# One query range for batch 0 and token groups of 6 and 8 blocks, in a ReLU-squared attention feeding a two-layer expert network

## The chip, the cores and the metric

One core of a Trainium2 chip. The metric is the device time of one execution in microseconds (us). A profile's span is some 1.5 to 2 us shorter than the time of the same kernel, so spans are compared only with spans and times only with times.

## The reference, cut to what matters

```python
batch, n_heads, seq, head_dim = 8, 12, 448, 64          # attention
scores = scale * (q @ k.T);  attn = relu(scores)**2 / S;  o = attn @ v
n_tokens, d_model, d_ff = 3584, 768, 2048               # expert network on the 8*448 tokens
h = x @ w_in;  g = h * sigmoid(1.702 * h);  out = g @ w_out
```

All inputs and the output are float32. The kernel computes in float16 with float32 sums.

Of the kernel before, what the change touches and what calls it, by code (L numbers as in the profile page):

```python
# [15 lines left out]
def kernel(  # L16
# [9 lines left out]
    nc = tc.nc  # L26
    B, H, S, D = q.shape
    NT, DM = out.shape
    DFF = moe_w_in.shape[1]
    J = S // 64  # L30
    NP = H // 4
# [9 lines left out]
    gblk = [4, 8, 8, 8, 6, 8, 6, 8]  # L41
    gcum = [0]
# [93 lines left out]


    def slots_of(q0, n):
        out_ = [[] for _ in range(n)]
        for j in range(J):  # L140
            lo = 0
            while lo < n:
                i, c = divmod(j * n + lo, J)
                hi = min(n, lo + J - c)
                out_[i].append((j, q0 + lo, q0 + hi, 64 * c))
                lo = hi
        return out_

    QA = gblk[0]
    split = slots_of(0, QA) + slots_of(QA, J - QA)  # L150
    whole = [[(j, 0, J, 0)] for j in range(J)]

    def pieces(u):
        return split if u < NP else whole

    early = []

    def scores(u, j, times=1):
        st = units[u]
        sc = early.pop() if early else ps_s.tile([128, 2, 512], F32, name="sc", tag="sc")  # L160
        for kb, q0, q1, c0 in pieces(u)[j] * times:
            for s in range(2):
                for a in range(2):
                    r = slice(64 * a, 64 * a + 64)
                    c = slice(64 * s, 64 * s + 64)
                    nc.tensor.matmul(  # L166
                        out=sc[c, a, c0:c0 + 64 * (q1 - q0)],
                        lhsT=st["kT"][r, kb, c],
                        rhs=st["qT"][r, q0:q1, c],
                        start=True, stop=True)  # L170
        return sc
# [14 lines left out]
    def av_mm(u, j, at):  # L186
        st = units[u]
        if "av" not in st:
            av = ps_s.tile([128, 2, 512], F32, name="av", tag="sc")
            st["av"] = [av[:, 0, :], av[:, 1, :]]  # L190
            st["pair"] = av
        base = QA if u < NP and j >= QA else 0
        for kb, q0, q1, c0 in pieces(u)[j]:
            for s in range(2):
                for a in range(2):
                    r = slice(64 * s, 64 * s + 64)
                    nc.tensor.matmul(  # L197
                        out=st["av"][s][64 * a:64 * a + 64, 64 * (q0 - base):64 * (q1 - base)],
                        lhsT=st["v16"][r, a, 64 * kb:64 * kb + 64],
                        rhs=at[r, a, c0:c0 + 64 * (q1 - q0)],  # L200
                        start=(kb == 0), stop=(kb == J - 1))
# [3 lines left out]
    def xt_evac(u, q0=0, q1=J):  # L205
        b, pr = divmod(u, NP)
        st = units[u]
        lo = b * J + q0
        while lo < b * J + q1:
            g = max(i for i in range(NG) if gcum[i] <= lo)  # L210
            hi = min(b * J + q1, gcum[g + 1])
# [3 lines left out]
            f = slice(64 * (lo - b * J - q0), 64 * (hi - b * J - q0))  # L215
# [204 lines left out]
    with tc.manual_schedule():  # L420
# [34 lines left out]
        def av(how, u, q0, q1):  # L455
            if "m" in how:
                units[u]["av"] = [ps_m.tile([128, 512], F32, name="avm", tag="mm")
                                  for _ in range(2)]
            for jj in range(q0, q1):
                av_mm(u, jj, ats.pop((u, jj)))  # L460
            xt_evac(u, q0, q1)

        def zeros(how, n):
            early.append(ps_s.tile([128, 2, 512], F32, name="sc", tag="sc"))
            for _ in range(n):
# [5 lines left out]
              "a": lambda how, u: av(how, u, 0, J if u >= NP else QA),  # L471
              "b": lambda how, u: av(how, u, QA, J),
# [11 lines left out]
            "jk0 jq0 z3 I jk1 k0 jq1 q0 k1 s0.0 jk2 jq2 s0.1 q1 x0.0 jv0 s0.2 jk4 jv2 k2 x0.1 "  # L484
            "s1.0 jv1 x0.2 jk3 s0.3 jq3 x1.0 s1.1 q2 z3 x0.3 x1.1 jw0 s1.2 s2.0 jv3 s1.3 x1.2 "
            "a0:m x2.0 x1.3 s2.1 s2.2 jw1 x2.1 s2.3 jq4 x2.2 a1:m s1.4 x2.3 s0.4 s0.5 x1.4 x0.4 "
            "a2:m x0.5 s1.5 x1.5 s0.6 jq5 x0.6 f0.0 s2.4 q3 s1.6 x2.4 k3 s2.5 jk5 s2.6:h f0.1 "
            "jw2 f0.2 x1.6 s3.0 x2.5 b1 x2.6 jv4 s3.1 b0:m jw3 x3.0 s3.2 x3.2 s3.3:h f0.3 x3.1 "
            "f0.4 jo0.1 f0.5 s3.4 x3.3 k4 x3.4 s3.5 jo0.0 s3.6 q4 G1 b2 q5 s4.0 jv5 x3.5 f0.6 "
            "x3.6 f0.7 x4.0 s4.1 x4.1 k5 a3 s4.2 f0.8 s4.3 x4.2 x4.3 f0.9 f0.10 L6 s4.4:d s4.5 "  # L490
            "x4.5 jo1.1 x4.4 s4.6:h f0.11 f0.12 s5.0 x4.6 s5.1 x5.0 x5.1 f0.13 a4 s5.2 s5.3:d "
            "f0.14 f0.15 s5.4 x5.3 x5.2 s5.5:d s5.6 x5.4 K6 x5.6 x5.5 m0.1.0 Q6 a5 m0.0.0 f1.0 "
            "f1.1 C1 C3 A2 R6 s6.0:h L7 E3 L8 jo1.0 s6.1 x6.1 A1 s6.2 Q7 C0 f1.2 f1.3 f1.4 s6.3 "
            "K7 C2 f1.5 x6.0 f1.6 R7 A3 f1.7 f1.8 E0 A0 L9 x6.2 x6.3 s6.4 x6.4 s6.5 s6.6 W6 K8 "
            "Q8 B0 B1 x6.5 E1 R8 x6.6 m0.1.1 s7.0 s7.1 B3 x7.0 s7.2 W7 x7.2 x7.1 m0.0.1 s7.3 a6 "
            "K9 s7.4:h x7.3 s7.5 f1.9 B2 s7.6:d f1.10 x7.6 x7.5 f1.11 x7.4 f1.12 s8.0 s8.1:d a7 "
            "s8.2:h Q9 s8.3 x8.0 x8.1 x8.3 W8 f1.13 f1.14 s8.4 R9 s8.5 x8.2 D2 s8.6:h x8.4 L10 "
            "x8.5 f1.15 W9 x8.6 p1.0.0 s9.0 a8 s9.1 E2 s9.2 p1.0.1 f2.0 f2.1 K10 x9.1 x9.0 L11 "
            "Q10 f2.2 x9.2 f2.3 D3 p1.0.2 p1.0.3 s9.3:h s9.4 R10 L12 D0 s9.5 f2.4 x9.4 K11 f2.5 "
            "f2.6 s9.6 Q11 x9.3 R11 x9.5 D1 s10.0:h W10 s10.1 p1.0.4 f2.7 L13 x9.6 f2.8 x10.0 "  # L500
            "x10.1 s10.2:d s10.3 a9 s10.4:h s10.5 x10.2 p1.0.5 x10.3 Q12 p1.0.6 f2.9 x10.4 "
            "x10.5 p1.2.0 p1.2.1 s10.6:d s11.0:h K12 x10.6 s11.1 L14 f2.10 p1.2.2 x11.0 f2.11 "
            "s11.2:d x11.1 a10 s11.3 W11 Q13 f2.12 x11.3 f2.13 x11.2 s11.4 Q14 K13 R12 L15 "
            "s11.5:d s11.6 p1.2.3 R13 p1.2.4 x11.6 x11.5 x11.4 f2.14 f2.15 s12.0 s12.1 a11 "
            "s12.2 K14 L16 p1.2.5 x12.2 p1.2.6 W12 p2.0.0 x12.0 W13 p2.0.1 Q15 x12.1 p2.0.2 "
            "s12.3:d s12.4:d s12.5 x12.3 f3.0 f3.1 f3.2 x12.4 K15 p2.0.3 p2.0.4 s12.6:d x12.5 "
            "L17 s13.0:h R14 s13.1 f3.3 x13.0 x12.6 f3.4 p2.0.5 p2.0.6 x13.1 s13.2 K16 s13.3 "
            "a12 K17 x13.2 W14 s13.4 p2.2.0 p2.2.1 s13.5 s13.6:h x13.3 x13.4 s14.0 x14.0 f3.5 "
            "Q16 p2.2.2 R15 x13.6 f3.6 W15 Q17 x13.5 f3.7 W16 f3.8 s14.1:d L18 a13 s14.2 x14.1 "
            "s14.3:h p2.2.3 f3.9 p2.2.4 x14.2 s14.4 x14.3 s14.5 x14.5 x14.4 R16 s14.6 x14.6 "  # L510
            "f3.10 f3.11 s15.0:d a14 s15.1 s15.2 f3.12 x15.0 Q18 f3.13 f3.14 R17 s15.3 x15.2 "
            "s15.4:h L19 x15.1 s15.5:d p2.2.5 x15.3 p2.2.6 x15.4 s15.6 x15.5 s16.0:h f3.15 f4.0 "
            "x16.0 f4.1 f4.2 f4.3 f4.4 p3.0.0 x15.6 p3.0.1 K18 s16.1:d s16.2:d a15 s16.3 x16.2 "
            "L20 x16.1 f4.5 f4.6 x16.3 f4.7 p3.0.2 s16.4 x16.4 s16.5 Q19 s16.6 f4.8 x16.5 K20 "
            "p3.0.3 s17.0 Q20 s17.1:h x16.6 f4.9 x17.1 f4.10 p3.0.4 x17.0 p3.0.5 W17 s17.2 a16 "
            "s17.3 x17.2 s17.4 f4.11 K19 s17.5:h x17.4 s17.6 x17.3 R18 p3.0.6 p3.2.0 x17.5 L21 "
            "x17.6 p3.2.1 p3.2.2 f4.12 s18.0 s18.1:d s18.2 f4.13 R19 p3.2.3 x18.0 p3.2.4 s18.3 "
            "x18.3 K21 s18.4:h x18.2 x18.1 L22 R20 a17 W18 f4.14 p3.2.5 p3.2.6 s18.5:d s18.6 "
            "f4.15 x18.6 f5.0 x18.5 i4.2.1 f5.1 x18.4 W19 s19.0:d s19.1:d x19.1 s19.2 x19.2 "
            "i4.2.0 K22 f5.2 W20 x19.0 f5.3 s19.3:d a18 s19.4:d s19.5:d Q21 p4.0.0 f5.4 p4.0.1 "  # L520
            "x19.5 f5.5 p4.0.2 Q22 x19.4 x19.3 f5.6 f5.7 s19.6 x19.6 s20.0:d s20.1 x20.0 R21 "
            "f5.8 f5.9 f5.10 s20.2 s20.3:d x20.1 a19 s20.4 x20.3 f5.11 x20.4 R22 p4.0.3 x20.2 "
            "p4.0.4 s20.5:d s20.6 x20.5 x20.6 s21.0:d W21 L23 f5.12 f5.13 s21.1 s21.2:h f5.14 "
            "f5.15 x21.1 x21.0 x21.2 p4.0.5 K23 s21.3 a20 s21.4 s21.5 p4.0.6 p5.0.0 x21.3 f6.0 "
            "f6.1 f6.2 x21.4 s21.6 s22.0:h x21.5 Q23 s22.1 f6.3 x22.1 f6.4 x21.6 f6.5 R23 x22.0 "
            "s22.2 a21 s22.3 s22.4 f6.6 x22.3 p5.0.1 f6.7 W22 f6.8 x22.2 p5.0.2 f6.9 x22.4 "
            "s22.5 x22.5 s22.6 s23.0:d f6.10 p5.0.3 W23 x22.6 p5.0.4 s23.1 s23.2 a22 x23.0 "
            "s23.3:h p5.0.5 x23.1 p5.0.6 s23.4:h x23.2 x23.3 s23.5 s23.6:d f6.11 p5.2.0 x23.6 "
# [41 lines left out]
```

## The kernel before: the parts that the change touches

A "unit" is four heads of one batch; there are 24 units, three to a batch. A "block" is 64 tokens, 7 to a batch, 56 in all. A "slot" is one key block of a unit: four score matmuls on 64x64 tiles of TensorE, a relu (ScalarE, or VectorE where marked `:d`) and a square (VectorE). The expert network runs on groups of blocks. The whole schedule is one list of words, issued in that order on every engine:

- `jk jq jv jw jo`: loads of k, q, v, w_in, w_out through GpSimd's queue; `k q`: transposes on TensorE with a copy on VectorE
- `s u.j`: scores and relu of slot j of unit u (`:t` issues the score matmuls twice, `:h` holds the relu back); `x`: its square; `a`, `b`: a unit's value product and its copy to the token tile
- `z3`: three filler matmuls of zeros; `I`: makes the identity matrix that the transposes need
- `f g.i`: matmuls of w_in for group g; `m`: one direct w_out product of 128 tokens; `p`: a paired product, 7 products of 8 matmuls for two token tiles in place of 8; `i`: the same tile alone; capitals: loads, casts and transposes of later units, and sums of weights

Before, batch 0 is computed in two query ranges, 4 blocks and 3 blocks, so that the first group of 4 blocks is ready early. Its slots are packed from pieces of different key blocks:

```python
gblk = [4, 8, 8, 8, 6, 8, 6, 8]
...
QA = gblk[0]
split = slots_of(0, QA) + slots_of(QA, J - QA)      # 10 + 9 pieces in 4 + 3 slots
whole = [[(j, 0, J, 0)] for j in range(J)]          # 7 pieces in 7 slots
...
for kb, q0, q1, c0 in pieces(u)[j] * times:         # pieces(u): split for units 0 to 2
    for s in range(2):
        for a in range(2):
            nc.tensor.matmul(out=sc[c, a, c0:c0 + 64 * (q1 - q0)],
                             lhsT=st["kT"][r, kb, c], rhs=st["qT"][r, q0:q1, c], ...)
```

Every matmul is two instructions of TensorE, a weight load and the matmul: the page counts 3392 of each.

## Time and profile before

| | before |
|---|---|
| time, median of 4 runs (lowest to highest) | 385.76 us (385.29 to 386.5) |
| span of the profile | 384.3 us |
| TensorE busy, matmuls | 370.9 us, 3392 |
| first expert matmul (word f0.0) starts | 23.80 us |
| clock at half | 24.2 to 27.6 us |
| waits of TensorE before 80 us that the profile names, over 0.8 us each, without the first (1.2 us, for the zeros of the fillers) | weight block 1.1, q of unit 6 0.9, and 1.2 with the cause "issue" |

"Issue" is time in which the engine waited for nothing that the profile shows; the prediction passed over that 1.2 us. It is one line of TensorE's order of time, in the middle of the value product of unit 2:

```profile
19.60 0.81 PE L197 MATMUL avm<-at,v 64*64 64x256 f16 x15
21.62 0.71 PE L197 MATMUL avm<-at,v 64*64 64x256 f16 x25 [1.21 <-issue]
```

(Start, duration, engine, line, operation, count, and in brackets the idle time before it and what ended it.)

### The profile page before, as it was taken

Reading aid. Unit: us, or ns where it says so; the run is one execution under the profiler, and the core shown is the slowest. Engines: PE = TensorE matmul, PEld = TensorE weight load, DVE = VectorE, ACT = ScalarE, POOL = GpSimd, SP = SyncE. Lnnn points to the kernel's source line nnn. Section 1 sums busy time; section 2 is a strip of 40 time slices with the busy share of each in tenths; the row PEclk is TensorE's granted clock in tenths of the full one; section 3 lists DMA queues with packets and bytes.
Section 4 is the critical chain, followed back from the end, with each engine's and each line's share of the span. In section 5 each row is a group of like instructions: output and inputs, shape, how many; then the busy total and the mean of one; then the engine's idle time right before and its main releaser. Section 6 shows DMA issues by size and latency. Waiting matters only on the chain.

```text
span 384.3 us, 8393 instructions
## 1 busy us (share of the span) xinstructions
PE 370.9 (97%) x3392; PEld 196.7 (51%) x3392; DVE 268.4 (70%) x442; ACT 210.4 (55%) x310; POOL 136.0 (35%) x200
## 2 busy tenths in 40 slices
PE   8779999999999999999999999999999999999994
PEld 4557653444545455544455555454455555555552
DVE  2878886797678879786768888587855867023473
ACT  1979855878684673585656755326567450232210
POOL 7618514816433351324433321343324220332100
PEclk9989999999999999999999999999999999999999
DMA  8999998996559878798432399365141331110333
GB/s 117 196 204 158 204 231 242 237 193 143 151 141 224 166 156 218 162 197 146 131 82 97 68 198 275 62 87 143 26 107 24 49 84 39 44 41 0 84 82 83
DMA packets 65222, 50.87 MB, mean 132 GB/s; under 512 B 35744, under 2 KB 61728, under 8 KB 65184
## 3 DMA queue, kind: packets, MB, share of 16 engines
q1 hardware_dynamic: 47872, 35.70, 38.0%
q0 software_dynamic: 17152, 14.55, 25.8%
q8 instruction: 26, 0.43, 0.4%
q10 hardware_dynamic: 160, 0.10, 0.1%
q14 instruction: 12, 0.10, 0.1%
HBM read 45.61 MB, written 11.01 MB: 147 GB/s over the span
## 4 chain that ended last, share of the span: by engine, by line
PE 84%; DMA 9%; DVE 2%; POOL 1%; issue 1%; ACT 1%; SPq 0%; ACTq 0%
PE ht L245 36%; PE op L310 29%; PE sc L166 8%; PE av L197 6%; DMA win<-in_moe_w_in_dram 3%; DMA wout<-in_moe_w_out_dram 3%; DMA qst<-in_q_dram 2%; PE op L271 1%; DVE osb L321 1%; PE zp L428 1%; DMA qT<-q 1%; PE tr L129 1%; ACT rl L180 0%; POOL k L119 0%; PE sc L466 0%
## 5 line engine op out<-in xcount | busy, mean ns | idle before, releaser
L245 PE MATMUL ht<-xt,win 128*128 128x512 f16 (+2 forms) x768 | 156.6, 353 | 1.2 <-DMA win<-in_moe_w_in_dram 1.1
L252 POOL TENSOR_SCALAR gt<-gf 128x512 f16<-128x512 f32 (+2 forms) x128 | 82.8, 647 | 206.4 <-ACT gf L250 200.6
L180 ACT ACTIVATE rl<-sc 128x896 f16<-128x896 f32 x138 | 121.8, 924 | 47.4 <-PE sc L166 38.4
L453 DVE TENSOR_TENSOR at<-rl 128x896 f16<-128x896 f16 x168 | 104.8, 651 | 20.9 <-ACT rl L180 20.1
L250 ACT ACTIVATE gf<-ht 128x512 f32<-128x512 f32 (+2 forms) x128 | 69.8, 547 | 86.4 <-PE ht L245 74.8
L245 PEld LDWEIGHTS <-win 128*128 128x128 f16 x768 | 72.1, 98 | 76.1 <-issue 13.9
L310 PEld LDWEIGHTS <-gt 128*128 128x128 f16 x424 | 40.6, 98 | 29.9 <-issue 3.4
L166 PE MATMUL sc<-qT,kT 64*64 64x448 f16 (+4 forms) x816 | 49.3, 327 | 2.6 <-ACT rl L180 1.0
L310 PEld LDWEIGHTS <-as 128*128 128x128 f16 x320 | 30.8, 98 | 23.5 <-issue 2.8
L310 PE MATMUL op<-wout,as 128*128 128x384 f16 x224 | 40.3, 326 | 0.0
L177 DVE TENSOR_SCALAR rl<-sc 128x896 f16<-128x896 f32 x30 | 32.2, 1085 | 11.1 <-PE sc L166 10.9
L310 PE MATMUL op<-wsum,gt 128*128 128x384 f16 x224 | 39.5, 326 | 0.0
L321 DVE SCALAR_TENSOR_TENSOR osb<-op,osb 128x384 f32<-128x384 f32 (+1 forms) x49 | 25.7, 545 | 14.9 <-PE op L310 14.6
L310 PE MATMUL op<-wout,gt 128*128 128x384 f16 (+1 forms) x200 | 35.3, 320 | 0.5 <-DVE osb L321 0.5
L197 PE MATMUL av<-at,v 64*64 64x448 f16 (+3 forms) x660 | 33.2, 336 | 0.0
L166 PEld LDWEIGHTS <-kT 64*64 64x64 f16 x816 | 19.3, 106 | 26.7 <-issue 20.6
L321 DVE SCALAR_TENSOR_TENSOR osb<-op,ea 128x384 f32<-128x384 f32 x24 | 13.3, 553 | 26.8 <-ACT eb L319 11.3
L217 DVE CAST xt<-av 128x768 f16<-128x768 f32 (+5 forms) x35 | 24.7, 735 | 8.5 <-PE av L197 8.4
L197 PEld LDWEIGHTS <-v 64*64 64x64 f16 x816 | 21.4, 107 | 12.6 <-issue 2.6
L305 DVE TENSOR_TENSOR as<-gt 128x1024 f16<-128x1024 f16 x38 | 26.1, 712 | 0.4 <-POOL gt L252 0.4
L104 POOL CAST q<-qst 128x896 f16<-128x896 f32 x18 | 16.9, 936 | 9.9 <-DMA qst<-in_q_dram 9.1
L91 POOL DMA_DIRECT2D v<-in_v_dram x24 | 18.0, 752 | 1.9 <-issue 0.6
(38 smaller groups left out, 170.0 us busy)
## 6 DMA issues: line engine op xcount, KB each, us to landing
out_dram<-osb SPq DMA_DIRECT2D x54, 192.0 KB, 2.9
kst<-in_k_dram SPq DMA_DIRECT2D x18, 448.0 KB, 4.0
qst<-in_q_dram SPq DMA_DIRECT2D x18, 448.0 KB, 4.7
v<-in_v_dram POOLq DMA_DIRECT2D x24, 224.0 KB, 5.2
win<-in_moe_w_in_dram POOLq DMA_DIRECT2D x8, 384.0 KB, 10.0
wout<-in_moe_w_out_dram POOLq DMA_DIRECT2D x4, 768.0 KB, 12.5
k<-in_k_dram POOLq DMA_DIRECT2D x6, 224.0 KB, 6.1
q<-in_q_dram POOLq DMA_DIRECT2D x6, 224.0 KB, 7.8
```

Source lines behind the costliest of these rows:

```text
L166: nc.tensor.matmul(out=sc[c, a, c0:c0 + 64 * (q1 - q0)], lhsT=st["kT"][r, kb, c], rhs=st["qT"][r, q0:q1, c], start=True, stop=True)
L177: nc.vector.tensor_scalar(out=rl, in0=sc[:, :, 0:S], scalar1=0.0, scalar2=None, op0=ALU.max)
L180: nc.scalar.activation(out=rl, in_=sc[:, :, 0:S], func=AF.Relu)
L197: nc.tensor.matmul(out=st["av"][s][64 * a:64 * a + 64, 64 * (q0 - base):64 * (q1 - base)], lhsT=st["v16"][r, a, 64 * kb:64 * kb + 64], rhs ...
L217: nc.vector.tensor_copy(out=xts[g][:, 2 * pr:2 * pr + 2, c], in_=st["pair"][:, :, f])
L245: nc.tensor.matmul(out=ht[:, 0:n], lhsT=w[:, kk, fo:fo + 128], rhs=xts[g][:, kk, 0:n], start=(kk == 0), stop=(kk == NK - 1))
L250: nc.scalar.activation(out=gf[:, 0:n], in_=ht[:, 0:n], func=AF.Gelu_apprx_sigmoid, scale=1.0 / SC)
L252: nc.gpsimd.tensor_scalar(out=gts[g][:, f, 0:n], in0=gf[:, 0:n], scalar1=SC, scalar2=1.0, op0=ALU.mult, op1=ALU.mult)
L305: nc.vector.tensor_tensor(out=out_, in0=x, in1=y, op=op)
L310: nc.tensor.matmul(out=op[:, 0:cw], lhsT=lhs[:, f, :], rhs=w[:, f, c0:c0 + cw], start=(start and f == 0), stop=(stop and f == HF - 1))
L321: nc.vector.scalar_tensor_tensor(out=o, in0=op[:, 0:w], scalar=sc, in1=add, op0=ALU.mult, op1=ALU.add)
L453: nc.vector.tensor_tensor(out=at, in0=rl, in1=rl, op=ALU.mult)
```

## The change

The intent is a simpler start: batch 0 like all others, in one query range with whole key blocks, and the groups 6, 8, 6, 8 and so on. The first group then needs all of batch 0's attention, less its last block. The list of words is a new one for the whole kernel.

```diff
-    gblk = [4, 8, 8, 8, 6, 8, 6, 8]
+    gblk = [6, 8] * (B // 2)
...
-        for kb, q0, q1, c0 in pieces(u)[j] * times:
-            for s in range(2):
+        for s in [0, 1] * times:
...                                             (the same in av_mm; xt_evac loses its query range)
-            "jk0 jq0 z3 I jk1 k0 jq1 q0 k1 s0.0 jk2 jq2 s0.1 q1 x0.0 jv0 s0.2 jk4 jv2 k2 x0.1 "
-            "s1.0 jv1 x0.2 jk3 s0.3 jq3 x1.0 s1.1 q2 z3 x0.3 x1.1 jw0 s1.2 s2.0 jv3 s1.3 x1.2 "
-            "a0:m x2.0 x1.3 s2.1 s2.2 jw1 x2.1 s2.3 jq4 x2.2 a1:m s1.4 x2.3 s0.4 s0.5 x1.4 x0.4 "
-            "a2:m x0.5 s1.5 x1.5 s0.6 jq5 x0.6 f0.0 s2.4 q3 s1.6 x2.4 k3 s2.5 jk5 s2.6:h f0.1 "
...                                             (35 lines cut)
+            "jq0 jk0 I q0 k0 z3 s0.0:d x0.0 s0.1 x0.1 jq1 jk1 s0.2 q1 s0.3 x0.2 x0.3 s0.4 k1 "
+            "x0.4 z3 jk4 jk2 s0.5 s0.6 k2 k4 x0.5 s1.0 s1.1 jv0 x0.6 s1.2 jq3 x1.0 x1.1 a0:m "
+            "s1.3 s1.4 x1.2 jq2 s1.5 jk3 q2 jk5 x1.3 x1.4 jv2 s1.6 x1.5 jv1 k3 s2.0:t q3 x1.6 "
+            "jw0 s2.1:t x2.1 s2.2:t x2.0 s2.3:t x2.2 a1:m x2.3 s2.4:t jq4 jq5 s2.5:t s2.6 x2.4 "
+            "x2.5 x2.6 jv3 jw1 jv4 k5 s3.0 jv5 a2 s3.1 q4 jw2 x3.0 x3.1 s3.2 f0.0 q5 x3.2 jw3 "
...                                             (34 lines cut)
```

## The prediction

The sum of the forecast came to +1.2 us, so 386.8 us, rounded to 386.5. Its unit costs are read from the trace of the kernel before (512, 384 and 256 columns 0.216, 0.1625 and 0.109 us apart; for the last, twelve take 1.48 us and six 0.83). The 2 us for three relu buffers in step c is the author's estimate, which no row shows.

> **What bounds the kernel now.** I read the page's busy table and slices first, then the stage table, then the order of time on TensorE and on VectorE, and the chain of waits last. "Slot" below means one key block's scores of one unit (four heads of one batch), its relu and its square. There are 24 units of 7 slots.
>
> ```profile
> PE 370.9 (97%) x3392; PEld 196.7 (51%) x3392; DVE 268.4 (70%) x442; ACT 210.4 (55%) x310; POOL 136.0 (35%) x200
> PE   8779999999999999999999999999999999999994
> DVE  2878886797678879786768888587855867023473
> ACT  1979855878684673585656755326567450232210
> PEclk9989999999999999999999999999999999999999
> ```
>
> TensorE is busy for 97% and is full in every slice but the first three and the last. So its work from the fourth slice on is on the path that sets the end, and only the first 30 us, where it has holes, can hide anything. The stage table shows what bounds that first stretch:
>
> ```profile
> core 0: us, PE busy (x) PEld busy (x) DVE busy (x) ACT busy (x) POOL busy (x), PEclk, DMA share, GB/s
> 10.00:20.00 10.00, 7.52 (x253) 5.45 (x249) 9.31 (x19) 9.91 (x14) 6.23 (x9) 1.00 1.25 198
> 20.00:30.00 10.00, 7.71 (x175) 5.55 (x177) 6.97 (x13) 7.61 (x11) 1.58 (x4) 0.83 1.25 205
> 30.00:40.00 10.00, 9.89 (x234) 7.04 (x225) 8.36 (x16) 9.22 (x16) 9.18 (x14) 1.00 1.01 158
> 50.00:60.00 10.00, 9.70 (x86) 5.17 (x84) 8.09 (x15) 3.44 (x5) 1.73 (x3) 1.00 1.00 208
> 60.00:70.00 10.00, 9.14 (x54) 3.84 (x53) 7.35 (x12) 7.51 (x12) 5.92 (x8) 1.00 1.05 265
> ```
>
> From 10 to 20 us ScalarE (9.91 of 10) and VectorE (9.31) are the full ones, with the loads running at about 200 GB/s beside them. From 20 to 30 us TensorE also loses clock (0.83). The chain of waits names the transfers that end last there:
>
> ```profile
> 12.22 11.44 DMA win<-in_moe_w_in_dram
> 23.80 1.13 PE ht L245 x6
> ...
> 48.49 9.56 DMA qst<-in_q_dram
> 58.11 0.94 POOL q L104
> 59.06 2.89 DMA qT<-q
> 62.09 0.76 PE sc L166 x12
> ```
>
> The first expert matmul (word f0.0) starts at 23.80, when the first weight block lands, after a wait of 1.1 us. The next wait is at 62.09: 0.9 us for the transposed q of unit 6.
>
> The unit costs of TensorE come from starts that follow each other in order of time:
>
> ```profile
> 349.23 1.46 PE L245 MATMUL ht<-xt,win 128*128 128x512 f16 x6
> 350.53 1.46 PE L310 MATMUL op<-wout,gt 128*128 128x384 f16 x8
> 351.83 4.05 PE L245 MATMUL ht<-xt,win 128*128 128x512 f16 x18
> ```
>
> Six 512-column matmuls take 350.53 - 349.23 = 1.30 us (0.216 each), and eight 384-column ones 351.83 - 350.53 = 1.30 us (0.1625 each). A whole slot's four 64x448 matmuls cost 0.189 us (the chain has 28 for a unit's value product in 1.32 us), a set of 14 transposes 0.52 us.
>
> [...] the six 256-column matmuls at 23.80 take 1.13 us, against 0.83 us for the six at 41.42, and the granted clock there is 0.83. [...] switches between 64x64 and 128x128 cost about 0.12 us each, worked out below. [...] 24 matmuls of 64 to 192 columns starting at 18.40 take 0.58 us, about 0.1 us for four, and so do four of 256 columns.
>
> **The change part by part.**
>
> *a. The split goes.* Units 0 to 2 did their attention in two query ranges (4 and 3 blocks). The pieces are 10 + 9 = 19 per unit instead of 7, at about 0.105 us: 2.0 us against 7 x 0.189 = 1.32, for scores and again for values. That saves 6 x 0.7 = 4.1 us of TensorE at most. The larger part lies before f0.0, in the holes. Nine of the 21 slots, and the three later value products, lie after it; I count 1.0 us on the path.
>
> *b. Groups 4,8,8,8,6,8,6,8 become 6,8 four times.* The first weight product keeps 3584 x 96 columns. The second pairs token tiles: 56 matmuls for two tiles, against 32 for one done alone. Before: 12 pairs, 2 singles, 2 direct = 672 + 64 + 64 = 800. After: 11 pairs, 3 singles, 3 direct = 616 + 96 + 96 = 808. Eight more at 0.1625 = +1.3 us, on the path.
>
> *c. The first group needs six blocks of batch 0 instead of four*, so all seven key blocks of all seven queries of units 0 to 2. From the listed order, before f0.0 stand 17 slots, 6 transpose sets and three partial value products before, and 24 slots, 11 sets and three whole ones after.
> VectorE sets this start, as an estimate from its rows and their starts. Up to the last copy of unit 2's values it has 21 squares (about 0.556 from start to start) = 11.7; 10 copies of transposes at 0.54 = 5.4; one relu 1.02; two value products copied in two halves of 448 (0.415 at 256 and 0.558 at 384 columns give some 0.535 start to start) = 2.1; one of 896, 1.03. The sum is 21.3 us from 7.59, plus 1.0 of holes seen at the start now: 29.9. ScalarE alone would reach 9.4 + 20 x 0.837 = 26.1, and the weight block (3.77 MB at the rates of the stage table) about 24 to 25. Three relu buffers tie ScalarE and VectorE together, both nearly full; I add 2 us for it. So f0.0 starts at 32, 8.2 us later than now.
> It then has more behind it. Useful TensorE work before f0.0, now: 6 x 0.52 + 17 x 0.189 + 12 slots' values 2.3 = 8.6 us. After: 11 x 0.52 + 24 x 0.189 + 21 x 0.189 = 14.2. Time that is not useful: 23.8 - 8.6 = 15.2 now, 32 - 14.2 = 17.8 after. Net +2.6 us. Doubled score matmuls (six slots marked for it, 1.1 us) lie in the holes and cost nothing.
>
> *d. From f0.0 to the value product of unit 6 (79.58 now).* Useful work now: by 79.58 12 x 0.52, 53 slots' scores and 42 slots' values at 0.189, 96 matmuls of 256 columns at 0.109, 54 at 0.216 and 64 at 0.1625 give 56.7; less 8.6 is 48.1 us, in 55.8. The 7.7 us lost are: the half clock at 23.8 to 28 about 1.6 (1.13 instead of 0.67, and likewise for the next five rows), the split 1.0, the q wait 0.9, and 4.2 of switches. After, the wait should go: the list puts three direct tiles (3 x 2.6 us) and two f words before unit 6's first slot, near 68 us, while its q is ready at about 62 (gate, load, cast and transpose as now). The split's 1.0 goes by (a). The clock dips as now.
>
> *e. Switches.* In 79.6 to 350 us useful work is 260.4 of 270.4, so 10 us are lost over the 80-odd mode switches of the list: 0.12 each. From unit 7's fourth slot on the lists have 84 and 86 switches: no difference. Between f0.0 and there they have 41 and 22, so up to 19 x 0.12 = 2.3 less. I take 0.8 of it, since the first weight blocks, the weight sums and the copies are as likely to open holes in the same stretch.
>
> Sum: +1.3 (b) + 2.6 (c) - 1.0 (a) - 0.9 (d) - 0.8 (e) = +1.2 us. On the measured median 385.6 that is 386.8; I round to 386.5.
>
> **The rivals.**
> 1. *TensorE starves longer at the start.* For: VectorE and ScalarE are already full from 10 to 20 us, and the new list doubles score matmuls from unit 2 on, which only makes sense where TensorE stands waiting. Each us that f0.0 comes after 32 adds nearly one: f0.0 at 37 gives 391 to 392. Against: the holes in ScalarE and VectorE from 20 to 30 us (7.61 and 6.97) show that a denser list has room.
> 2. *The new list is simply tighter.* If VectorE runs as in the sum without the 2 us, all 19 saved switches count, and the doubled scores keep the clock up (1.6), the sum is 386.8 - 2 - 1.5 - 1.6 = 381.7. For: 128 runs of one mode in the list against 135. Against: a denser 30 to 60 us has less slack for late transfers.
> 3. *A transfer takes the place of the wait removed.* The third and fourth w_in blocks are issued behind the first group's activations; I expect them at 37 and 41, used at about 45 and 51. If the order on the queue shifts by some 10 us, a hole of 2 to 3 us appears: 389.
>
> **Range and chances.** The two large unknowns are the start of f0.0 (some 3 us either way) and the holes up to 80 us (2 to 3); the rest of the kernel is the same kind of full TensorE. That gives 382 to 392. Two per cent is 7.7 us: faster would need nearly every loss before 80 us to go (2%), slower a start like rival 1 and a missed transfer (7%), within 91%.
>
> **What would show it.** Step b: 808 matmuls of the second product. Step a: 672 value matmuls, 696 score matmuls. Step c: f0.0 at 30.5 to 33, VectorE over 90% busy before it. Step d: no wait of unit 6's scores for its q. Step e: equal pace from unit 7 on, and the same tail of some 6 us. I am wrong if f0.0 comes after 35, if TensorE has over 3 us of holes between f0.0 and 80 us, or if the later stretch differs by more than 2 us.

## The result, and the profile after

| | before | after |
|---|---|---|
| time, median of 4 runs (lowest to highest) | 385.76 us (385.29 to 386.5) | 382.78 us (382.41 to 383.24) |
| span of the profile | 384.3 us | 380.7 us |
| TensorE's instructions in the program (two for each of 3392 and 3136 matmuls, and two more) | 6786 | 6274 |
| w_out matmuls (the last eight are done as two halves of 192 columns each, counted once here; the trace has 808 and 816) | 800 | 808 |
| f0.0 starts | 23.80 us | 28.60 us |
| clock at half before the end | 24.2 to 27.6 us | never |

The ratio of the times is 0.9922, with a 95% interval of 0.9901 to 0.9942: 0.8% shorter. The time lies in the predicted range, 0.8 us above its lower end, but the forecast leaned to slower and the kernel became faster.

The page of the changed kernel, the same rows as shown of before:

```profile
PE 370.2 (97%) x3136; PEld 193.3 (51%) x3136; DVE 256.5 (67%) x425; ACT 214.6 (56%) x314; POOL 136.0 (36%) x200
PE   8889999999999999999999999999999999999994
DVE  2999763778958986566778874638777865313374
ACT  2987753786776768367564556476764461242210
PEclk9999999999999999999999999999999999999999
```

TensorE is busy for 0.7 us less in a span that is 3.6 us shorter. The work is nearly the same, the holes are fewer. The table by stage (busy us of TensorE, weight loads, VectorE, ScalarE, GpSimd, then the granted clock, the share of the transfer engines, GB/s):

```profile
10.00:20.00 10.00, 8.33 (x159) 4.84 (x158) 9.90 (x21) 9.07 (x12) 6.47 (x11) 1.00 1.23 191
20.00:30.00 10.00, 8.89 (x162) 5.34 (x160) 10.00 (x21) 9.12 (x12) 4.12 (x6) 1.00 1.25 206
30.00:40.00 10.00, 10.00 (x118) 5.12 (x112) 9.06 (x14) 7.74 (x13) 6.40 (x10) 1.00 1.24 205
50.00:60.00 10.00, 10.00 (x80) 5.49 (x79) 4.00 (x7) 3.64 (x7) 4.49 (x7) 1.00 1.20 237
60.00:70.00 10.00, 10.00 (x61) 4.73 (x59) 5.16 (x8) 4.86 (x7) 3.59 (x5) 1.00 0.89 225
```

Compare the second row with before's: VectorE 10.00 in place of 6.97, ScalarE 9.12 in place of 7.61, TensorE 8.89 in place of 7.71 at a full clock in place of 0.83, and 162 matmuls in place of 175. The start is denser on all three, with fewer and larger matmuls. From 30 us on TensorE has no hole in any of these rows. The waits of TensorE that are left:

```profile
PE tr L129 <- DVE xt L197: 1.3, 2, 0.6
PE zp L405 <- DVE zero L402: 1.2, 1, 1.2
PE sc L145 <- ACT rl L159: 0.7, 2, 0.4
PE tr L129 <- DVE kT L133: 0.5, 1, 0.5
PE op L287 <- DVE osb L298: 0.5, 1, 0.5
```

(Who waited for whom; us in total, times, longest.) The waits for the weight block, for unit 6's q and the one without a cause are gone.

The account further down rests on two more readings, with the columns of the table by stage. In the changed kernel VectorE is full from its first relu to f0.0:

```profile
8.25:28.60 20.35, 17.27 (x330) 10.13 (x322) 20.21 (x40) 18.50 (x22) 12.34 (x18) 1.00 1.24 197
```

In the kernel before TensorE is busy for less than half of the time just before its clock falls at 24.2 us:

```profile
20.00:21.00 1.00, 0.41 (x13) 0.25 (x13) 0.94 (x2) 1.00 (x3) 0.00 (x0) 1.00 1.26 205
21.00:22.00 1.00, 0.38 (x24) 0.38 (x27) 0.63 (x1) 0.79 (x1) 0.00 (x0) 1.00 1.23 202
22.00:23.00 1.00, 0.72 (x40) 0.51 (x29) 0.70 (x3) 0.44 (x1) 0.00 (x0) 1.00 1.26 204
23.00:24.00 1.00, 0.20 (x2) 0.22 (x3) 1.00 (x3) 1.00 (x2) 0.00 (x0) 1.00 1.24 204
```

Where the 3.6 us of span came from, with the prediction's own measure, useful TensorE work from the lists at the same unit costs against time gone by:

| stretch | before: time, useful, lost | after: time, useful, lost | lost, difference |
|---|---|---|---|
| start to f0.0 | 23.8, 8.6, 15.2 | 28.6, 14.2, 14.4 | -0.8 |
| f0.0 to unit 6's value product (79.58; 78.53) | 55.8, 48.1, 7.7 | 49.9, 47.3, 2.6 | -5.1 |
| from there to the end | 304.7, 288.4, 16.3 | 302.2, 284.9, 17.3 | +1.0 |
| w_out work (8 more matmuls) | | | +1.3 useful |

The sum is -3.6 us. The last stretch differs by 1.0 us in one profile each, which no run here explains.

### The profile page after: what moved, and what is told of

The parts are those of the page before. It is cut to its first block, busy times and chain, and to the rows that moved or that the text cites. A ratio compares the mean times of both kernels' runs of the same rounds, so it can differ in the third digit from the quotient of the medians.

```text
span 380.7 us, 7864 instructions
## 1 busy us (share of the span) xinstructions
PE 370.2 (97%) x3136; PEld 193.3 (51%) x3136; DVE 256.5 (67%) x425; ACT 214.6 (56%) x314; POOL 136.0 (36%) x200
## 4 chain that ended last, share of the span: by engine, by line
PE 90%; DVE 7%; issue 1%; ACT 1%; ACTq 0%
PE ht L222 39%; PE op L287 29%; PE sc L145 9%; PE av L174 7%; PE op L248 4%; DVE at L430 3%; DVE osb L298 1%; PE zp L405 1%; DVE kT L133 1%; PE tr L129 1%; DVE xt L197 1%; DVE qT L133 1%; DVE rl L156 0%; ACT eb L296 0%; ACT rl L159 0%
## 5 line engine op out<-in xcount | busy, mean ns | idle before, releaser
L222 PE MATMUL ht<-xt,win 128*128 128x384 f16 (+1 forms) x768 | 156.3, 353 | 0.4 <-ACT gf L227 0.4
L229 POOL TENSOR_SCALAR gt<-gf 128x384 f16<-128x384 f32 (+1 forms) x128 | 82.6, 645 | 201.6 <-ACT gf L227 196.5
L159 ACT ACTIVATE rl<-sc 128x896 f16<-128x896 f32 x144 | 126.2, 917 | 41.9 <-PE sc L145 33.5
L227 ACT ACTIVATE gf<-ht 128x384 f32<-128x384 f32 (+1 forms) x128 | 69.6, 546 | 85.9 <-PE ht L222 76.4
L145 PE MATMUL sc<-qT,kT 64*64 64x448 f16 x696 | 48.6, 357 | 1.2 <-ACT rl L159 0.7
L298 DVE SCALAR_TENSOR_TENSOR osb<-op,osb 128x384 f32<-128x384 f32 (+1 forms) x45 | 23.6, 544 | 23.6 <-PE op L287 23.3
L156 DVE TENSOR_SCALAR rl<-sc 128x896 f16<-128x896 f32 x24 | 26.1, 1087 | 16.1 <-PE sc L145 15.8
L174 PE MATMUL av<-at,v 64*64 64x448 f16 x616 | 33.2, 350 | 0.2 <-DVE at L430 0.2
L287 PE MATMUL op<-wout,gt 128*128 128x384 f16 (+1 forms) x184 | 32.4, 319 | 0.5 <-DVE osb L298 0.5
L194 DVE CAST xt<-av 128x896 f16<-128x896 f32 (+2 forms) x32 | 24.5, 793 | 11.6 <-PE av L174 11.6
L145 PEld LDWEIGHTS <-kT 64*64 64x64 f16 x696 | 17.2, 105 | 24.9 <-issue 17.2
L174 PEld LDWEIGHTS <-v 64*64 64x64 f16 x672 | 19.8, 107 | 12.8 <-issue 2.8
L104 POOL CAST q<-qst 128x896 f16<-128x896 f32 x18 | 17.3, 959 | 8.4 <-issue 7.5
```

The source lines that it names most:

```text
L145: nc.tensor.matmul(out=sc[c, a, 0:S], lhsT=st["kT"][r, j, c], rhs=st["qT"][r, :, c], start=True, stop=True)
L156: nc.vector.tensor_scalar(out=rl, in0=sc[:, :, 0:S], scalar1=0.0, scalar2=None, op0=ALU.max)
L159: nc.scalar.activation(out=rl, in_=sc[:, :, 0:S], func=AF.Relu)
L174: nc.tensor.matmul(out=st["av"][s][64 * a:64 * a + 64, 0:S], lhsT=st["v16"][r, a, 64 * j:64 * j + 64], rhs=at[r, a, :], start=(j == 0), st ...
L194: nc.vector.tensor_copy(out=xts[g][:, 2 * pr:2 * pr + 2, c], in_=st["pair"][:, :, f])
L222: nc.tensor.matmul(out=ht[:, 0:n], lhsT=w[:, kk, fo:fo + 128], rhs=xts[g][:, kk, 0:n], start=(kk == 0), stop=(kk == NK - 1))
```

## The experiments

Times below are the mean of a run's fast runs less that of the kernel before in the same rounds; the changed kernel stands at -3.0 us on this scale. The first runs asked which parts of the new start carry the gain: the place of the filler matmuls, the doubled scores, VectorE, the pieces, the groups.

### Fillers ahead of the first transposes again

```diff
-            "jq0 jk0 I q0 k0 z3 ...
+            "jq0 jk0 z3 I q0 k0 ...
```

> The changed kernel, with one thing put back: the three filler matmuls of zeros stand before the first transposes again (and the identity matrix is made between them), as in the kernel before. Theory S (VectorE sets when the first expert matmul f0.0 starts, from its first copy on, and TensorE then runs full to the end): VectorE's first copy starts about 0.8 to 1.0 us later, f0.0 at 29.4 to 29.6 in place of 28.6, and the time is 0.8 to 1.0 us longer than the changed kernel's. Rival R (the start has slack, the gain over the kernel before is less work and fewer mode switches on TensorE): f0.0 moves by less than 0.3 us and so does the time.

Measured: 382.92 us, ratio 0.9926, -2.9 us. f0.0 at 28.61 us. The rival's "no difference" held, but the profile did not test its reason (and the times cannot tell less than their intervals of 0.8 us): VectorE's first copy started at 6.61 us, as in the changed kernel (6.60), and its second at 7.16 (7.14). The second set of transposes waits for the load of k, which landed at 6.27 us here and at 6.30 there, and the fillers cost little here, since TensorE's full clock was granted from 5.0 us on. That instant differs from profile to profile, from 4.3 to 7.1 us (6.44 in the changed kernel's), with no relation to the list that they show. The 7.59 us that the prediction took from the kernel before is a late draw of it: full clock came at 7.09 us there, the three fillers started 0.43 us apart in place of 0.21, and the first transposes, behind them, began at 6.88 us although their load had landed at 5.09, as early as in any profile.

### The doubled scores left out

```diff
-    ... s2.0:t ... s2.1:t ... s2.2:t ... s2.3:t ... s2.4:t ... s2.5:t
+    ... s2.0 ... s2.1 ... s2.2 ... s2.3 ... s2.4 ... s2.5
```

> The changed kernel without the doubling of six score slots of unit 2 (24 matmuls fewer, 1.1 us of TensorE work). Theory C (the doubled scores keep TensorE dense enough that its clock isn't halved when the experts start): the granted clock falls to 0.5 for about 3 us somewhere between 20 and 32 us, as in the kernel before, and the time is 1.0 to 1.6 us longer. Rival (they lie in holes and the clock would hold anyway): clock 1.00 throughout, time within 0.3 us. Third possibility: they are in the way of the start, and without them f0.0 comes up to 0.5 us earlier.

Measured: 383.38 us, ratio 0.9933, -2.5 us; the granted clock is 1.00 in all stages up to the end. In this profile f0.0 came at 29.83 us, after waits of 2.0 us in all for loads of k that the changed kernel's profile does not have. The doublings neither keep the clock up (Theory C, which rested on the one fall at 24.2 us in the kernel before) nor cost anything that these runs can tell from noise (0.5 us between two intervals of 0.8 to 0.9 us half-width).

### Doubled scores in the kernel before

```diff
-    ... s0.4 s0.5 ... s1.5 ... s0.6
+    ... s0.4:t s0.5:t ... s1.5:t ... s0.6:t
```

> The kernel before, with the scores of four slots (units 0 and 1, the last before f0.0) doubled, nothing else. Theory C: TensorE's clock, which falls to 0.5 from 24.4 to 27.4 us, holds at 1.0; the 1.6 us that the six instruction groups of that stretch lost come back, the time is 1.2 to 1.6 us shorter than the kernel before. Rival: the clock falls in spite of it, since the hole of 1.1 us ahead of f0.0 and the one of 1.2 us before it remain, and the time is within 0.3 us.

Measured: 389.38 us, ratio 1.0083, +3.2 us. Neither theory had this time. The clock still fell, as the rival said, but twice (21.8 to 25.2 and 28.6 to 32.0 us), and TensorE stood still twice without a cause in the profile:

```profile
21.88 0.53 PE L166 MATMUL sc<-qT,kT 64*64 64x128 f16 x9 [1.87 <-issue]
28.61 0.31 PE L129 MATMUL tr<-ident,q 128*64 128x128 f16 x1 [1.65 <-issue]
```

The second stop is before the last of 14 transposes whose inputs are the same tile. Data cannot be what the last one lacked. That made a new theory necessary.

### First transposes ahead of the fillers in the kernel before

```diff
-            "jk0 jq0 z3 I jk1 k0 jq1 q0 k1 ...
+            "jk0 jq0 I k0 q0 z3 jk1 jq1 k1 ...
```

> The kernel before, with the first transposes put ahead of the three filler matmuls of zeros, as the changed kernel has them. Theory S says of the kernel before that f0.0 waits there for the weight block's transfer (landed at 23.67), not for VectorE: VectorE's first copy starts 0.8 to 1.0 us earlier, but f0.0 stays at 23.3 to 23.9 and the time moves by less than 0.4 us. Rival: the earlier start by itself is worth what it is worth in the changed kernel, 0.8 to 1.0 us shorter.

Measured: 385.87 us, ratio 1.0003, +0.1 us. f0.0 at 24.17 us after 1.7 us of waiting for the weight block: outside the stated 23.3 to 23.9, but the time did not move, as expected. The order within the first words is worth nothing in either kernel that these runs can tell (0.1 us, with intervals of 0.8 to 1.0 us half-width).

### More work on VectorE

```diff
-            nc.vector.tensor_tensor(out=at, in0=rl, in1=rl, op=ALU.mult)
+            for _ in range(2 if "w" in how else 1):          # x0.4 x1.1 x1.4 x2.1 marked w
+                nc.vector.tensor_tensor(out=at, in0=rl, in1=rl, op=ALU.mult)
```

> The changed kernel, with four of the squares before f0.0 (in units 0, 1 and 2) done twice on VectorE: the same values, 4 x 0.56 = 2.2 us more of VectorE. Theory S (VectorE sets f0.0): f0.0 at 30.4 to 30.9 in place of 28.6 and the time 1.8 to 2.2 us longer. Rival R (ScalarE or the transfers set it, VectorE has slack): f0.0 moves by less than 1 us, and what it moves is made up later; time within 0.5 us.

Measured: 384.98 us, ratio 0.9981, -0.7 us, so 2.3 us more than the changed kernel. f0.0:

```profile
30.86 1.15 PE L222 MATMUL ht<-xt,win 128*128 128x384 f16 x6
```

28.60 became 30.86: 2.26 us later for 2.2 us of added VectorE work, and all of it arrives at the end. VectorE is on the path up to f0.0, and nothing after it absorbs a delay.

### The split's arithmetic in the new order

```diff
+    QA = 4                                         # pieces of 4 and 3 blocks for units 0 to 2, 19 per unit
-        base = QA if u < NP and j >= QA else 0
+        base = 0                                   # both ranges into one tile: VectorE's work is unchanged
```

(On the kernel before, with the new groups and the new list.)

> The changed kernel with the arithmetic of batch 0 in two query ranges again (4 and 3 blocks: 19 pieces per unit and product in place of 7), in the changed order, with the same work on VectorE and ScalarE. It shows what the smaller pieces cost by themselves, about 4 us of TensorE work by my count. Theory S (TensorE has holes before f0.0, and all of it lies there): time longer by 0 to 0.8 us. Rival R (TensorE's work counts there too): 2.5 to 4 us longer.

Measured: 392.67 us, ratio 1.0181, +7.0 us: 10 us more than the changed kernel, with the same list and the same work on VectorE and ScalarE. Both theories are far off; 4 us of array time cannot cost 10. TensorE's order of time has four stops without a cause and f0.0 at 37.80 us:

```profile
15.14 1.30 PE L197 MATMUL avm<-at,v 64*64 64x256 f16 x61 [0.50 <-issue]
...
21.40 0.35 PE L129 MATMUL tr<-ident,k 128*64 128x128 f16 x5 [2.39 <-issue]
...
27.32 1.00 PE L197 MATMUL avm<-at,v 64*64 64x64 f16 x47 [1.15 <-issue]
...
33.26 2.66 PE L197 MATMUL av<-at,v 64*64 64x256 f16 x72 [2.42 <-issue]
...
37.80 1.72 PE L245 MATMUL ht<-xt,win 128*128 128x384 f16 x6
```

Numbering TensorE's instructions in the program and counting the matmuls in the trace up to each stop gives the same place every time: 223 matmuls and instruction 448, 351 and 704, 479 and 960; the fourth stop is at 606 recorded matmuls, two instructions short of 1216, which one missing record explains. These are 192 + 256, + 512, + 768, + 1024. The stop of the kernel before is at instruction 704 too, and so is the first of the kernel before with doubled scores; its second is at 960.

The page has a transfer queue called "instruction". Its line in part 3, of the kernel before and of the changed one:

```profile
q8 instruction: 26, 0.43, 0.4%
```
```profile
q8 instruction: 24, 0.39, 0.4%
```

(Packets, MB, share.) In the trace each packet is 16384 bytes. 6786 and 6274 instructions, less the first 192, are 25.8 and 23.8 times 256, and the queue has 26 and 24 packets: so I read a packet as one block of 256 instructions of TensorE, with the stops at the edges of the blocks. The times of the packets fit:

| split in the new order: packet on the instruction queue | 12.7 to 13.6 | 18.8 to 19.8 | 25.1 to 26.0 | 31.0 to 31.9 |
|---|---|---|---|---|
| TensorE resumes after the stop | 15.14 | 21.40 | 27.32 | 33.26 |

TensorE resumes 1.3 to 1.6 us after each packet has landed. The next packet starts 3.5 to 3.7 us after it resumed. One round is some 6.1 us, and in that time TensorE can use 128 matmuls. In the changed kernel the packet of 22.5 to 23.5 us is landed well before TensorE reaches instruction 704, between 25 us (306 matmuls) and 30 us (392). There, too, the packets start only after TensorE has passed an edge, 2.4 to 2.9 us after it (448, 704 and 960 passed at 19.60, 27.28 and 37.69 us, packets at 22.5, 29.7 and 40.2), so at these three edges the supply is not more than one block ahead. In the kernel before, instruction 704 is reached at 20.4 us, its packet landed at 20.1, and TensorE resumes at 21.62.

Theory I is that reading. The next runs test it.

### Many small matmuls against few large ones

Both without `:t`, in 18 slots before f0.0:

```diff
+        if extra == "y":                       # many: sixteen matmuls of 64 columns, the same values again
+            for s in [0, 1] * 4:
+                for a in range(2):
+                    nc.tensor.matmul(out=sc[c, a, 0:64], lhsT=st["kT"][r, j, c],
+                                     rhs=st["qT"][r, 0:1, c], start=True, stop=True)
```
```diff
+        if extra == "y":                       # few: two matmuls of zeros of 512 columns
+            for a in range(2):
+                nc.tensor.matmul(out=sc[:, a, :], lhsT=zero[:, 0:128], rhs=zero[:, 0:512], ...)
```

> Theory I (new, from the runs so far): TensorE's own instructions come in blocks of 16 KB, 256 instructions, over a transfer queue of their own; while the loads fill the transfer engines a block takes about 6 us to arrive, so TensorE can use at most some 128 matmuls (a weight load and a matmul each) per 6 us, and stands still at the block's edge if it needs more. The split's small pieces do that. Here: the changed kernel without its six doublings, and in 18 of the slots before f0.0 sixteen more matmuls of 64 columns on 64x64 tiles (the same values again), 288 in all or 576 instructions; at about 0.026 us each that is 0.42 us of TensorE a slot, 7.5 us in all. Theory I: stops of 1 to 2.5 us each with no cause in the trace, at instructions 704, 960 and 1216 of TensorE's stream (192 and a multiple of 256), f0.0 at 36 to 39 in place of 28.6, time 8 to 11 us longer than the changed kernel. Rival W (what counts is TensorE's array time): f0.0 at 31 to 33 and no such stops, time as in the next run.

> The same array time in few instructions: the changed kernel without its six doublings, and in the same 18 slots two matmuls of zeros of 512 columns on the whole array (0.43 us a slot, 7.8 us in all, 36 matmuls or 72 instructions). Theory I: no stops without a cause, f0.0 at 29 to 32 (part of the 7.8 us fits into the holes), time 0.5 to 3 us longer than the changed kernel. Rival W: the same f0.0 and time as in the run with many small matmuls, within 1 us.

Measured: many 388.55 us, ratio 1.0067, +2.5 us, f0.0 at 34.96; few 388.15 us, ratio 1.0054, +2.0 us, f0.0 at 34.15. The places of the stops came as Theory I said (instructions 448, 704, 960, and 1216 but for the same missing record), with 1.55, 2.32, 0.99 and 1.33 us; the few large matmuls have none. The times missed, and f0.0 with them, on both sides: 5.5 us more than the changed kernel for the many in place of 8 to 11, and 5.0 for the few in place of 0.5 to 3. The large ones filled TensorE itself (10.00 busy of 10 from 10 to 30 us), so only some 2 to 3 of their 7.8 us fitted into holes. And a small matmul takes far less array time than the 0.026 us I had assumed, an estimate (a quarter of the prediction's 0.105 us per piece of four matmuls); in the next run 128 of them take 1.24 us, 0.0097 each. So this pair shows where the stops come from, but its times do not tell the theories apart.

### Instructions alone, with the transfer engines idle

```diff
+        for _ in range(225):                   # after the last word: 900 matmuls of 64 columns
+            for s in range(2):
+                for a in range(2):
+                    nc.tensor.matmul(out=bt[c, a, 0:64], lhsT=ident[r, c], rhs=ident[r, 0:64], ...)
```

> The changed kernel with 900 matmuls of 64 columns on 64x64 tiles after everything else, when the loads are long over and only the last store is in flight: 1800 instructions, seven blocks. It measures how fast TensorE's instructions can arrive when nothing else uses the transfer engines. Theory I: blocks follow each other by less than 4.5 us, and each stop at a block's edge is under 1 us or there is none[...]. Rival (a block takes some 6 us whatever the load): 7 blocks x 6 = 42 us or more.

Measured: 402.81 us in one look. TensorE's order of time at the end:

```profile
375.82 2.19 PE L520 MATMUL burst<-ident 64*64 64x64 f16 x147
379.32 1.24 PE L520 MATMUL burst<-ident 64*64 64x64 f16 x128 [1.30 <-issue]
383.32 1.72 PE L520 MATMUL burst<-ident 64*64 64x64 f16 x128 [2.76 <-issue]
387.05 1.93 PE L520 MATMUL burst<-ident 64*64 64x64 f16 x128 [2.01 <-issue]
390.78 1.92 PE L520 MATMUL burst<-ident 64*64 64x64 f16 x128 [1.80 <-issue]
```

Exactly 128 matmuls from stop to stop, with no load and no wait; the last stores end at 380 us, so from the second stop on hardly anything else moves. Rounds of 3.5 to 4.0 us, so the stated "under 4.5" held and "6 us whatever the load" is out; the stops are 1.3 to 2.8 us, longer than stated, since 128 of these matmuls run in 1.24 us at the full clock. So the supply of TensorE's instructions is one block per 3.7 us or so when the transfer engines are idle, and one per 6.1 us during the loads of the start. The packets show where the difference lies: a packet takes 0.9 to 1.4 us in both cases, and TensorE resumes 1.3 to 1.6 us after it has landed, but it starts 1.0 to 1.7 us after TensorE resumed here, and 3.5 to 3.7 us after it under the loads.

### The split with fewer loads

```diff
+        if u >= NP:                            # load16: batch 1 takes the tiles of batch 0 (wrong result)
+            st[n + "16"] = units[u - NP][n + "16"]
+            return
-    ... jw1 ... jw2 ... f0.0 q5 ...
+    ... f0.0 jw1 jw2 q5 ...
```

> The kernel with the changed order and the split arithmetic (the one that stopped at 19.0, 26.1 and 30.9 us and started f0.0 at 37.8), with fewer loads: batch 1's q and k are not loaded (its units take the tiles of units 0 to 2, so the result is wrong on purpose), and the second and third weight block are asked for only after f0.0. The transfer engines then run dry from some 22 us until f0.0. Theory I: the stops after 22 us shrink to under 0.5 us or vanish, f0.0 at 29 to 33. Rival (the stops come from the small pieces themselves or from the sequencer): stops at the same instructions, of the same length, f0.0 after 35.

Measured in one look, with a wrong result on purpose: f0.0 at 33.30 us, just outside the stated 29 to 33, in place of 37.80. The transfer engines fell to 44 GB/s from 20 to 30 us. The stops at 448 (0.40 us) and 704 (2.29 us) are there as before, when the loads still ran; at 960 and 1216 there are none. The packets, 5.8 us apart until 19.0, follow then at 22.6, 26.9 and 30.7 us, 3.6 to 4.3 apart. Same instructions, same pieces, no stops once the loads are gone: it is the supply under load. (The clock was at half from 20.7 to 27.5 us here, so TensorE was slow up to instruction 960. But the 128 matmuls from there to 1216 ran in 3.4 us, 27.09 to 30.51, with no stop, which one block per 6.1 us does not allow. The half clock and the two stops left are the likely reason that f0.0 still comes 4.7 us after the changed kernel's; no run separates them.) (The time, 390.89 us, says nothing: the late weight block cost 3.5 us later.)

### The old groups with the new start

```diff
-    gblk = [6, 8] * (B // 2)
+    gblk = [4, 8, 8, 8, 6, 8, 6, 8]            # new list up to unit 6's value product, then the old order
```

> A mixture: the changed kernel's list and its one query range up to the value product of unit 6 (without the third direct token tile), but the groups 4, 8, 8, 8, 6, 8, 6, 8 and, from there on, the order of the kernel before. It tells the start apart from the groups. If the whole gain of the change comes from the start and the eight extra matmuls of the new groups cost 1.3 us: 1.3 to 2.2 us shorter than the changed kernel, that is 4.3 to 5.2 shorter than the kernel before. If the new groups carry part of the gain (six-block groups give longer stretches between the slots, so fewer holes before unit 7): as long as the changed kernel or longer.

Measured: 394.73 us, ratio 1.0211, +8.4 us. f0.0 at 28.25, as it should be, but then:

```profile
61.12 0.76 PE L145 MATMUL sc<-qT,kT 64*64 64x448 f16 x12 [1.86 <-DMA qT<-q]
82.29 4.74 PE L248 MATMUL op<-wout,gt 128*128 128x384 f16 x16 [5.25 <-DMA wout<-in_moe_w_out_dram]
```

TensorE waits 1.9 us for unit 6's q and 5.2 us for w_out, and its clock falls to half for 10 us around them (62.4 to 65.8 and 79.5 to 86.3 us). I read it so that with a first group of 4 blocks TensorE has less work between the loads and runs into them. That is in favour of "the groups carry part of the gain", but the joined list was never arranged for these groups, and a better one might hide those transfers. The run does not settle it.

### An attempt at a faster version

```diff
-    ... s0.0:d ... k5 s3.0 ... f0.0 q5 ...
+    ... s0.0 ... s3.0 ... f0.0 q5 k5 ...
```

> The changed kernel with 1.6 us taken off VectorE before f0.0: the first slot's relu goes to ScalarE (1.09 us of VectorE), and the transposes of unit 5's k, with their copy of 0.55 us, move behind f0.0. Theory S (VectorE sets f0.0): f0.0 at 27.2 to 28.0 in place of 28.6, time 0.6 to 1.4 us shorter than the changed kernel. Rival: ScalarE (18.5 of 22 us busy there) or the weight block's landing takes over as the bound, and the gain is under 0.4 us.

Measured: 383.36 us, ratio 0.9934, -2.6 us: no gain over the changed kernel. f0.0 at 28.50 us in place of 28.60. Taking 1.6 us off VectorE gives nothing, adding 2.2 us costs 2.2: VectorE (20.1 of the 20.25 us from 8.25 to 28.5 in the changed kernel) and ScalarE (18.4) are both near full, and here they stand at 18.7 and 19.0. The trace shows where the freed time went: VectorE now waits 1.44 us, to 8.98 us, for the first relu, now on ScalarE, and at the end 0.48 us for unit 2's value product. So VectorE is not the only bound: relieved of this work, it waits for the others. No kernel of the study beats the changed one.

## Why the prediction was right or wrong

The range held and "within 2%" was right, but not for the reasons given: the errors of the sum come to 4.8 us, nearly all one way, and a range 10 us wide took them in. The direction was wrong, and with it the main path of the sum: +1.2 us predicted, -3.6 us of span measured. Rival 2 ("the new list is simply tighter", 381.7) came closest.

- **Step b was right:** 808 matmuls, +1.3 us.
- **Step c failed most: 3.4 us of the error.** Predicted: f0.0 at 32 and +2.6 us net. Measured: 28.60, outside the 30.5 to 33 that was to show it, and -0.8. The count of VectorE's work, 21.3 us, was right in sum: VectorE is busy for 21.37 of the 22.0 us from its first copy to f0.0. (Its 0.535 us for a copy of 448 columns does not follow from the two figures beside it; the copies of one such product took 1.19 us in place of 1.07.) VectorE was on the path: it is busy 20.21 of the 20.35 us from 8.25 to 28.60, and the run with four more squares moved f0.0 by just what was added. It was not alone there, as the attempt at a faster version shows. The terms added to the count were wrong. The 2 us for three relu buffers tying two full engines together did not appear; the 1 us of early holes was 0.6; and the start at 7.59 us belonged to fillers at half the clock, ahead of the first transposes, and was 6.60 in the changed kernel's profile. 2.0, 0.4 and 1.0 are the 3.4 us.
- **Step d was wrong on the clock.** "The clock dips as now" cost 1.6 us in the sum; there was no dip. In the kernel before TensorE is busy for only 1.7 of the 4 us from 20 to 24, behind the stop at instruction 704 and the wait for the weight block, and the clock halves at 24.2 us. The changed kernel's TensorE has no such stretch, and in the other profiles with stops, too, the clock's falls come during a stop or within 2.6 us of its end, though not every stop brings one; no run shows more of the cause. (The working "1.13 instead of 0.67" sets a duration against a spacing; the duration at full clock is 0.83. The size holds all the same, since 3.4 us at half clock lose 1.7.) It is not the doubled scores that prevent it, as rival 2 supposed: without them the clock holds too, and in the kernel before they make it worse. The rest of d was right: unit 6's q is no longer waited for.
- **Steps a and e were mis-sized.** In e, I took 0.8 of 2.3 us for 19 fewer mode switches out of caution. All 41 switches before were put at 4.2 us of loss; in the changed kernel the whole loss of that stretch is 2.6 us with 22 switches, which fits 0.12 each with nothing else lost. (In the chain of the kernel before, six 512-column matmuls take 1.40 us behind scores on 64x64 tiles, at 125.35, and 1.29 behind a w_out product, at 120.76; twelve score matmuls ahead of such a switch take 0.69 us, at 124.66, where 28 value matmuls take 1.32.) The clock's 1.6, the wait's 0.9 and 2.3 for the switches make 4.8 of the 5.1 us by which that stretch improved; no run takes them one by one. In a, 0.105 us per piece was a misreading: the 0.58 us of "24 matmuls" includes the tail of the last one, some 0.2 us (of 64 columns, lasting 0.189 us). Matmuls of 64 columns on four tiles run at 128 in 1.24 us, 0.039 us for four. In the trace before, four of 192 columns follow each other in 0.082 to 0.086 us, where 192/448 of 0.189 is 0.081: these pieces cost hardly more than their columns in the array. Its count behind f0.0 was off too: by the list 17 of the 21 slots stand before f0.0, so the scores of four lie after it, not of nine.
- **What the prediction did not have at all** is what pieces really cost here: instructions. The split has 288 more matmuls in its 3 units, 576 instructions, more than two blocks of 6.1 us each while the loads run. In the old list that shows as one stop of 1.2 us and the clock lost behind it; in the new, denser list the same pieces cost 10 us (four stops of 6.5 us together and 10 us at half clock). With pieces the new start is 7 us slower than the kernel before; so whole key blocks are a condition of its gain. That part is shown. How much a list of its own for one query range would gain with the old groups is not, since the mixture that was to show it waited for its weights.

## What to carry to other kernels

Splitting a matmul into narrow pieces can be free in the array and still not free: count TensorE's instructions against the supply, which was here 256 per 6.1 us with the loads at 200 GB/s and per 3.7 us or so with idle transfer engines, and look for it behind "issue" waits that come every 256 instructions (0.4 to 2.8 us here). Waiting longer for a first group with more work in it need not lose against an early small one when the other engines have holes in the meantime: here it went with a gain, as part of a whole new list, and its own share is not shown. When a start is estimated as the sum of a full engine's work, don't add an allowance for coupling that no row shows, and don't take the instant of its first instruction from one profile (the first copy started anywhere from 5.8 to 7.6 us).
